# A delta rule before routed experts: chunks of 32 tokens with four heads on the partitions, the inverse by substitution on VectorE

## The chip, the core and the metric

One of the eight cores of a Trainium2 chip runs the whole program. The metric is the device time of one execution in microseconds (us), the median of three runs. A core has five engines with queues of their own: TensorE (PE; its weight loads are listed as PEld), VectorE (DVE), ScalarE (ACT), GpSimd (POOL) and SyncE (SP, which here only issues transfers). Each takes its instructions in order and waits at semaphores for the others.

## The reference

The first part is a linear attention with a delta rule, for 4 batch rows, 8 heads, 768 tokens and 48 columns a head; the second gives each of the 3072 tokens to one of 8 experts by a hash of its id. All is float32.

```python
k_n = k / (np.linalg.norm(k, axis=-1, keepdims=True) + 1e-06)
state = np.zeros((B, H, D, D))
for t in range(S):
    kt, vt, bt = k_n[:, :, t], v[:, :, t], beta[:, :, t, None]
    y[:, :, t] = np.einsum('bhd,bhde->bhe', q[:, :, t], state)
    v_old = np.einsum('bhde,bhd->bhe', state, kt)
    state = state + bt[:, :, :, None] * np.einsum('bhd,bhe->bhde', kt, vt - v_old)
x = y.transpose(0, 2, 1, 3).reshape(B * S, H * D)
expert_idx = token_ids * 2654435761 % E
for e in range(E):
    mask = expert_idx == e
    out[mask] = np.maximum(x[mask] @ w1[e], 0.0) @ w2[e]
```

## The kernel before, in words

**The delta rule** takes the tokens in chunks of 128. For one head and chunk, with L[t, s] = k_t . k_s for s < t and S0 the state ahead of the chunk, W solves (I + L diag(beta)) W = V - K S0; then Y = Q S0 + stril(Q K^T) diag(beta) W and S1 = S0 + (diag(beta) K)^T W. A unit is a chunk of one batch row with its 8 heads, and there are 24 units. Two generators work on a unit:

- `invert(n)` (L298) does what does not depend on the state. It normalises K on POOL (L308, L321), transposes K, Q and beta K on TensorE (L333), forms the two triangular products (L347, masked by VectorE at L350), and then builds the 128x128 inverse T of each head by doubling: six levels, from blocks of 2 rows to blocks of 128. A level is a product of all 8 heads into the PSUM tile `inv` (L367), masked by VectorE (L375), a second product evicted by ScalarE (L379), and a transpose (L372) evicted by ScalarE.
- `step(n)` (L403) does what depends on the state: psK = K S0 (L410), V - psK on VectorE (L418), W = T (V - K S0) (L423), the state's increment psS (L431), Y in psY (L410, L438), and the store of 128 token rows of Y to the DRAM tensor `x_scratch` (L447).

The loop at L456 interleaves two `invert` generators with one `step` and with the routing, which turns the token ids into the token of each expert slot (`gidx`). A scheduler then moves instructions between neighbouring stages, so an engine's final order is not the order of the code; each engine's queue keeps that final order.

**The experts** (L479 to L583) begin when the stores have landed. For each expert four indirect loads gather 128 token rows from `x_scratch` (L490), TensorE transposes them (L499), and two products with the expert's weights follow (L506 and L517); POOL scatters the rows (L521). Weights come by SP (L67, L69); the first expert's load stands at the middle of the delta rule, the next three behind its end.

The level of the doubling, which the change takes out, reads:

```python
Y = wk.tile([P, H, P], F32, tag="Y", bufs=2)
by_head(Y, product(LK, T), masked(i))
T = wk.tile([P, H, P], F32, tag="T", bufs=3)
by_head(T, product(TT, Y), copy)
TT = wk.tile([P, H, P], F32, tag="TT", bufs=3)
by_head(TT, transposed(T), copy)
```

## Time and profile before

| | |
|---|---|
| median of three runs | 1319.23 us (1318.14 to 1320.88) |
| the profiled execution: first to last instruction | 1317.1 us |
| what the median lies above that span | 2.1 us |
| TensorE matmul busy | 1268.8 us, 96% |
| TensorE weight loads busy | 1078.0 us, 82% |
| VectorE busy | 445.7 us, 34% |
| ScalarE busy | 403.9 us, 31% |
| GpSimd busy | 219.8 us, 17% |
| end of the delta rule's last eviction | 951.7 us |
| transfers | 54.94 MB, 42 GB/s over the span |

The profile is of one execution. The busy time of an engine is the union of its instructions; idle time is put down to whatever released the engine. The profiled execution's own device time is not listed apart from its span, so the span is compared with the median of the runs.

### The profile page before, as it was taken

To read this page: it belongs to the slowest core of one execution; us is meant where nothing else is said; L and a number is where in the kernel's file an instruction comes from. 1 tells how busy PE (TensorE), PEld (TensorE's weight loads), DVE (VectorE), ACT (ScalarE), POOL (GpSimd) and SP (SyncE) were. 2 spreads that over 40 slices of the span, in tenths; PEclk is the share of its full clock that TensorE was granted. 3 is DMA by queue.
4 is the path that set the end of the run, shared out by engine and by line. 5 is a ranking of instruction groups with operands and counts; after the bars stand their busy time and mean duration, and the time that the engine had idled before them with its cause. 6 is when DMAs were issued, how large, how long until landed. Compare 5 with 4: busy or idle time off the path is not lost. (4 is left out here: it accounts for less than half of the span.)

```text
span 1317.1 us, 20472 instructions
## 1 busy us (share of the span) xinstructions
PE 1268.8 (96%) x8730; PEld 1078.0 (82%) x8730; DVE 445.7 (34%) x926; ACT 403.9 (31%) x745; POOL 219.8 (17%) x214
## 2 busy tenths in 40 slices
PE   5899999999999999999999999999879999999997
PEld 4899999999999999999999999999835555555554
DVE  7734334343434443343444334333121111111110
ACT  1343444344343434434343443434300000000000
POOL 5402011110201111020111101011042211220011
PEclk9999999999999999999999999999979999999999
DMA  9001010111101011110100000000093232310000
GB/s 218 14 18 32 7 31 13 25 25 25 26 7 25 19 26 25 25 25 7 25 13 19 13 7 7 1 7 7 13 346 127 83 114 67 135 34 12 6 20 17
DMA packets 94236, 54.94 MB, mean 42 GB/s; under 512 B 77434, under 2 KB 88774, under 8 KB 94144
## 3 DMA queue, kind: packets, MB, share of 16 engines
q1 hardware_dynamic: 89856, 44.05, 12.4%
q0 software_dynamic: 4096, 9.45, 2.1%
q8 instruction: 69, 1.13, 0.4%
q14 instruction: 23, 0.19, 0.0%
q10 hardware_dynamic: 192, 0.12, 0.0%
HBM read 45.74 MB, written 11.01 MB: 43 GB/s over the span
## 5 line engine op out<-in xcount | busy, mean ns | idle before, releaser
L375 DVE TENSOR_TENSOR Y<-inv,masks 128x512 f32<-128x512 f32 x288 | 197.4, 691 | 254.0 <-PE inv L367 253.4
L367 PE MATMUL inv<-T,LK 128*128 128x128 f32 x2304 | 279.4, 276 | 3.0 <-DVE T L375 3.0
L367 PEld LDWEIGHTS inv<-T,LK 128*128 128x128 f32 x2304 | 268.3, 193 | 3.5 <-DVE T L375 3.5
L379 ACT ACTIVATE T<-inv 128x512 f32<-128x512 f32 x240 | 143.3, 597 | 343.1 <-PE inv L367 343.1
L367 PE MATMUL inv<-Y,TT 128*128 128x128 f32 x1920 | 235.7, 276 | 2.9 <-DVE Y L375 2.9
L367 PEld LDWEIGHTS inv<-Y,TT 128*128 128x128 f32 x1920 | 227.5, 192 | 5.9 <-ACT root L313 1.9
L517 PE MATMUL o_ps<-w_sb,h_sb 128*128 128x384 f32 x512 | 169.9, 486 | 0.0
L506 PE MATMUL h_ps<-xT,w_sb 128*128 128x512 f32 x384 | 168.0, 598 | 0.0
L506 PEld LDWEIGHTS h_ps<-xT,w_sb 128*128 128x128 f32 x384 | 73.7, 192 | 91.1 <-issue 89.2
L517 PEld LDWEIGHTS o_ps<-w_sb,h_sb 128*128 128x128 f32 x512 | 95.2, 190 | 61.1 <-issue 1.0
L379 ACT ACTIVATE TT<-inv 128x512 f32<-128x512 f32 x240 | 128.5, 600 | 28.7 <-PE inv L372 28.2
L372 PE MATMUL inv<-ident,T 128*128 128x128 f32 x960 | 122.7, 274 | 0.1
L321 POOL TENSOR_TENSOR KN<-Ku,rn 128x384 f32<-128x384 f32 x24 | 19.9, 828 | 555.3 <-PE psT L333 549.9
L372 PEld LDWEIGHTS inv<-ident,T 128*128 128x128 f32 x960 | 108.0, 143 | 1.7 <-ACT T L379 1.6
L347 PE MATMUL psG<-KQT,BT 128*128 128x256 f32 x384 | 95.3, 391 | 1.9 <-DVE LQ L350 1.1
L347 PEld LDWEIGHTS psG<-KQT,BT 128*128 128x128 f32 x384 | 70.0, 194 | 13.2 <-PE inv L367 1.1
L509 ACT ACTIVATE h_sb<-h_ps 128x512 f32<-128x512 f32 x32 | 19.1, 597 | 183.5 <-PE h_ps L506 162.4
L511 DVE TENSOR_SCALAR h_sb<-h_ps 128x512 f32<-128x512 f32 x32 | 22.1, 692 | 145.3 <-PE h_ps L506 145.3
L490 POOL DMA_INDIRECT xg<-x_scratch,gidx x32 | 32.7, 1021 | 208.4 <-PE xT_ps L499 151.2
L385 POOL TENSOR_TENSOR TT<-LK,mask_t 128x1024 f32<-128x1024 f32 x24 | 57.8, 2410 | 1.9
L521 POOL DMA_INDIRECT out_dram<-o_sb,gidx x32 | 32.0, 1001 | 136.4 <-ACT o_sb L520 87.4
L520 ACT COPY o_sb<-o_ps 128x384 f32<-128x384 f32 x16 | 7.6, 478 | 142.4 <-PE o_ps L517 142.4
(129 smaller groups left out, 1010.8 us busy)
## 6 DMA issues: line engine op xcount, KB each, us to landing
w_sb<-in_moe_w_dram SPq DMA_DIRECT2D x16, 1536.0 KB, 7.3
Ku<-in_k_dram SPq DMA_DIRECT2D x24, 192.0 KB, 3.2
Q<-in_q_dram SPq DMA_DIRECT2D x24, 192.0 KB, 3.4
Vu<-in_v_dram SPq DMA_DIRECT2D x24, 192.0 KB, 4.3
x_scratch<-x_sb SPq DMA_DIRECT2D x24, 192.0 KB, 1.9
xg<-x_scratch,gidx POOLq DMA_INDIRECT x32
out_dram<-o_sb,gidx POOLq DMA_INDIRECT x32
bt<-in_beta_dram ACTq DMA_DIRECT2D x1, 96.0 KB
```

What stands on the lines that cost most here:

```text
L321: nc.gpsimd.tensor_tensor(KN[:, :, 0:D], Ku, rn.broadcast_to([P, H, D]), op=ALU.mult)
L347: nc.tensor.matmul(psG[:, hh], lhsT=BT[:, j, hh, :], rhs=KQT[:, :, j, :], start=(hh == 0), stop=True, skip_group_check=True)
L367: return lambda ps, h, first: nc.tensor.matmul(ps, lhsT=lhsT[:, h, :], rhs=rhs[:, h, :], start=first, stop=True, skip_group_check=True)
L372: return lambda ps, h, first: nc.tensor.transpose(ps, t[:, h, :], ident)
L375: return lambda dst, ps: nc.vector.tensor_tensor(dst, ps, masks[:, i].broadcast_to([P, HB, P]), op=ALU.mult)
L379: nc.scalar.activation(dst, ps, ACT.Copy)
L385: nc.gpsimd.tensor_tensor(TT, LK, mask_t.broadcast_to([P, H, P]), op=ALU.mult)
L490: nc.gpsimd.indirect_dma_start(out=xg, out_offset=None, in_=x_dram[:, :], in_offset=bass.IndirectOffsetOnAxis(ap=idx, axis=0), bounds_chec ...
L506: nc.tensor.matmul(h_ps[:, :width], lhsT=w1_sb[:, co, fo * P:(fo + 1) * P], rhs=xT[:, co, :width], start=(co == 0), stop=(co == CO - 1))
L511: nc.vector.tensor_scalar(out=h_sb[:, fo, :width], in0=h_ps[:, :width], scalar1=0.0, scalar2=None, op0=ALU.max)
L517: nc.tensor.matmul(o_ps, lhsT=h_sb[:, fo, col * P:(col + 1) * P], rhs=w2_sb[:, fo, :], start=(fo == 0), stop=(fo == FO - 1))
L521: scat = nc.gpsimd.indirect_dma_start(out=out[:, :], out_offset=bass.IndirectOffsetOnAxis(ap=idx, axis=0), in_=o_sb, in_offset=None, bound ...
```

## The change

The delta rule is written anew, the experts are kept.

- A chunk is 32 tokens and holds all 32 (batch row, head) pairs: a tile of 128 partitions is four heads of 32 tokens, and there are NT = 8 such tiles a chunk and NU = 24 chunks. In K4 and Q4 (32 tokens x 4 heads on the partitions) a tile has two column blocks of 48, and a head fills the one of its parity, so that a product of K4 transposed serves two heads.
- `prepare(c)` loads and normalises K, transposes K4 and Q4 (16 transposes), adds column blocks on POOL (`side`), and makes in 8 matmuls the products with K and Q. The K products go by ScalarE into NT, the Q products masked by VectorE into MT. One bank, `psG`, holds them.
- `invert(g)` serves four chunks (GC = 4). A 32x32 block transpose on VectorE puts one (head, chunk) on each of the 128 partitions, with its 32x32 matrix along the free axis. Then 31 rounds of a multiplication into tmp and an addition to U build the inverse by substitution; a second block transpose gives TU.
- `step(c)` copies TU into the block diagonal TB, and takes two halves of four tiles through psK, R2, psW, W2, psS and psY. The state accumulates in PSUM (`psS`), and ScalarE copies it out after each half.
- Loads are four a tensor and chunk, each of 32 partitions; K has 7 buffers, Q and V 3. A chunk's rows are stored by four transfers. The rows of `x_scratch` stand in the order (token, batch row), and `gx` is the index tile for the gathers.
- beta comes by 16 small loads on POOL's queue. The first expert's weights are loaded when the last `prepare` is done.

The core of the diff:

```diff
-            for i in range(1, LEVELS):
-                Y = wk.tile([P, H, P], F32, tag="Y", bufs=2)
-                by_head(Y, product(LK, T), masked(i))
-                yield
-                if i < LEVELS - 1:
-                    T = wk.tile([P, H, P], F32, tag="T", bufs=3)
-                    by_head(T, product(TT, Y), copy)
-                    yield
-                    TT = wk.tile([P, H, P], F32, tag="TT", bufs=3)
-                    by_head(TT, transposed(T), copy)
-                    yield
...
+        for t in K4s[:4]:
+            nc.gpsimd.memset(t, 0.0)
...
+        for i in range(4):
+            for j in range(GC):
+                p0 = C * i + NT * j
+                nc.gpsimd.dma_start(out=beta_i[p0:p0 + NT], in_=beta_r[i, j])
...
+        def prepare(c):
+            K4, Q4 = K4s[c % NB], Q4s[c % 3]
+            if c >= 4:
+                load_k(c, nc.sync)
+            if c >= 3:
+                load_q(c, nc.sync)
+            ksq = pre.tile([P, NT, 2 * D], F32, tag="ksq", bufs=1)
+            nc.scalar.activation(ksq, K4.rearrange("p t r d -> p t (r d)"), ACT.Square)
...
+            nc.gpsimd.tensor_tensor(K4v, K4v, rn.broadcast_to([P, NT, 2 * D]), op=ALU.mult)
+            yield
+            for a, (src, dst) in enumerate(((K4, KTs[c]), (Q4, QTs[c]))):
+                for h in range(2):
+                    psT = ps_t.tile([2 * D, HT, P], F32, tag="t")
+                    for i in range(HT):
+                        nc.tensor.transpose(
+                            psT[:, i, :], src[:, HT * h + i].rearrange("p r d -> p (r d)"), ident)
+                    own = dst[:, HT * h:HT * h + HT]
+                    nc.scalar.activation(own, psT, ACT.Copy)
+                    by_r = own.rearrange("p t (u r c) -> p (t u) r c", u=2, r=2)
+                    nc.gpsimd.tensor_tensor(side[:, HT * h:HT * h + HT, a], by_r[:, :, 0],
+                                            by_r[:, :, 1], op=ALU.add)
+            yield
+            for h in range(2):
+                psG = ps_g.tile([P, 2, HT, 2 * C], F32, tag="g")
+                for i in range(HT):
+                    nc.tensor.matmul(
+                        psG[:, :, i, :], lhsT=KTs[c][:, HT * h + i],
+                        rhs=side[:, HT * h + i].rearrange("p a u c -> p a (u c)"),
+                        start=(i == 0), stop=True, skip_group_check=True)
+                for p in range(2):
+                    nc.scalar.activation(
+                        NTs[c // GC][pair(p), :, x0:x0 + HT].rearrange("p t x -> p x t"),
+                        psG[pair(p), 0, :, p * C:(p + 1) * C], ACT.Copy)
+                nc.vector.tensor_tensor(
+                    MTs[c][:, HT * h:HT * h + HT].rearrange("p t (u r c) -> p (t u) r c", u=2, r=2),
+                    psG[:, 1].rearrange("p t (u c) -> p (t u) c", u=2)[:, :, None, :]
+                    .to_broadcast([P, 2 * HT, 2, C]),
+                    mask.rearrange("p t (u r c) -> p (t u) r c", u=2, r=2), op=ALU.mult)
+                yield
+        def invert(g):
+            Ni = wk.tile([P, C, C], F32, tag="Ni", bufs=1)
+            nc.vector.transpose(Ni, NTs.pop(g))
+            nc.vector.tensor_tensor(Ni, Ni, nbeta[:, g, None, :].to_broadcast([P, C, C]),
+                                    op=ALU.mult)
+            U = wk.tile([P, C, C], F32, tag="U", bufs=1)
+            nc.gpsimd.memset(U, 0.0)
+            nc.gpsimd.tensor_copy(U.rearrange("p c i -> p (c i)")[:, ::C + 1], beta_i[:, g])
+            yield
+            for j in range(C - 1):
+                n, m = j + 1, C - 1 - j
+                tmp = wk.tile([P, C * C // 4], F32, tag="tmp", bufs=2, name="tmp")
+                tmp = tmp[:, 0:n * m].rearrange("p (n m) -> p n m", n=n)
+                nc.vector.tensor_tensor(tmp, U[:, 0:n, j:j + 1].to_broadcast([P, n, m]),
+                                        Ni[:, j:j + 1, j + 1:].to_broadcast([P, n, m]),
+                                        op=ALU.mult)
+                nc.vector.tensor_tensor(U[:, 0:n, j + 1:], U[:, 0:n, j + 1:], tmp, op=ALU.add)
+                yield
+            nc.vector.transpose(TUs[g].rearrange("p x i -> p i x"), U.rearrange("p c i -> p i c"))
+            yield
+        def step(c):
+            for i in range(4):
+                nc.vector.tensor_copy(TB[quarter(i), :, i, :], TUs[g][quarter(i), x0:x0 + NT, :])
+            yield
+            for h in range(2):
+                if c > 0:
+                    for i in range(HT):
+                        nc.tensor.matmul(psK[:, i], lhsT=KTs[c][:, t0 + i], rhs=S0[:, i],
...
+                for p in range(2):
+                        nc.vector.tensor_tensor(R2[pair(p), :, p], V[pair(p), t0:t0 + HT],
+                                                psK[pair(p), :, p], op=ALU.subtract)
...
+                for i in range(HT):
+                    nc.tensor.matmul(psW[:, i], lhsT=TB[:, t0 + i], rhs=R2[:, i],
...
+                nc.scalar.activation(W2, psW, ACT.Copy)
+                yield
+                if c < NU - 1:
+                    for i in range(HT):
+                        nc.tensor.matmul(psS[h][:, i], lhsT=K4s[c % NB][:, t0 + i], rhs=W2[:, i],
...
+                    nc.scalar.activation(S1, psS[h], ACT.Copy)
+                    states[h] = S1
+                yield
+                if c > 0:
+                    for i in range(HT):
+                        nc.tensor.matmul(psY[:, i], lhsT=QTs[c][:, t0 + i], rhs=S0[:, i],
...
+                for i in range(HT):
+                    nc.tensor.matmul(psY[:, i], lhsT=MTs[c][:, t0 + i], rhs=W2[:, i],
...
+        for c in range(NU):
+            todo = [step(c)]
+            if c + AHEAD < NU:
+                todo.append(prepare(c + AHEAD))
+                todo.append(parts(route, 1))
+            if c % GC == GC - 1:
+                todo.append(inv)
+            else:
+                todo.append(parts(inv, 12))
+            run(*todo)
+            if (c + AHEAD) % GC == GC - 1 and c + AHEAD < NU:
+                inv = invert((c + AHEAD) // GC)
```

The final order of three queues shows where the new work stands. On TensorE before, in the middle of the delta rule, the products of the inverse (`inv`, of one or the other of two units) surround the steps (psK, psW, psS, psY):

```order
L372 MATMUL inv<-ident,T 128x128 x8
L410 MATMUL psK<-Sbd,KQT 128x96 x4
L367 MATMUL inv<-T,LK 128x128 x8
L423 MATMUL psW<-Rn,last 128x48 x8
L367 MATMUL inv<-Y,TT 128x128 x8
L431 MATMUL psS<-W,BK_90 128x96 x4
L410 MATMUL psY<-Sbd,KQT 128x96 x4
L438 MATMUL psY<-W,LQ 128x48 x8
```

On TensorE with the change, around the first product with a new inverse (psW of chunk 12, which reads TB), stand only `prepare` of two later chunks (psT, psG) and the step itself:

```order
L433 MATMUL psK<-S_2752,KT 128x96 x4
L359 MATMUL psT<-ident,K_2_89 96x128 x8
L359 MATMUL psT<-ident,Q_1_102 96x128 x8
L375 MATMUL psG<-side,KT 128x2x64 x8
L444 MATMUL psW<-R_0_94,TB_98 128x96 x4
L461 MATMUL psY<-S_2752,QT 128x96 x2
```

What moved: the products of the inverse are gone from TensorE, and ahead of psW it has one `prepare` left to do. On VectorE with the change, the start of that same substitution, behind the last mask of the chunk that it waited for; before, VectorE had only masks and subtractions of single instructions here, such as `L375 TENSOR_TENSOR Y<-inv,masks 128x512 x6`:

```order
L384 TENSOR_TENSOR MT<-psG,mask 128x512
L394 STREAM_TRANSPOSE Ni<-NT 128x1024
L395 TENSOR_TENSOR Ni<-Ni,nbeta 128x1024
L437 TENSOR_TENSOR R_0_94<-V,psK 64x4x48
L405 TENSOR_TENSOR tmp<-U,Ni 128x31
L408 TENSOR_TENSOR U<-U,tmp 128x31
L405 TENSOR_TENSOR tmp<-U,Ni 128x60
L437 TENSOR_TENSOR R_0_94<-V,psK 64x4x48
L408 TENSOR_TENSOR U<-U,tmp 128x2x30
L405 TENSOR_TENSOR tmp<-U,Ni 128x87
```

A chain of 62 small instructions stands there now, with the subtractions of half a step inside it. On POOL with the change, the start of the program, where before a dozen memsets and the identity stood ahead of the first work on K:

```order
L116 MEMSET K_3_90 128x768
L153 DMA beta_i<-in_beta_dram 8x6x32 x16
masks.py:197 MEMSET ident 128x128
L165 MEMSET K_4_91 128x768
masks.py:199 ISA
masks.py:199 AFFINE_SELECT ident<-ident 128x128
L165 MEMSET K_5_92 128x768
L165 MEMSET K_6_93 128x768
```

Sixteen loads stand ahead of the identity now; seven more memsets and two index tiles (L167, L171) follow before the first normalisation of K (L348).

## Rows read from the trace of the kernel before

**Rows 1.** The page: busy us of the engines, TensorE's clock in 40 slices.

```profile
PE 1268.8 (96%) x8730; PEld 1078.0 (82%) x8730; DVE 445.7 (34%) x926; ACT 403.9 (31%) x745; POOL 219.8 (17%) x214
PEclk9999999999999999999999999999979999999999
```

**Rows 2.** Busy time by stage: stretch, us, each engine, clock, DMA share, GB/s.

```profile
0.00:952.00 952.00, 923.66 (x7738) 896.87 (x7738) 394.98 (x838) 377.14 (x697) 155.08 (x150) 1.00 0.11 24
952.00:1317.00 365.00, 345.14 (x992) 181.09 (x992) 50.73 (x88) 26.75 (x48) 64.72 (x64) 0.97 0.25 87
```

**Rows 3.** The same of instructions on the tile inv alone, first stage.

```profile
0.00:952.00 952.00, 678.69 (x5760) 657.34 (x5760) 228.34 (x336) 295.17 (x528) 1.00 0.11 24
```

**Rows 4.** Timeline of TensorE's weight loads: start us, us, line, operation, count.

```profile
601.34 1.78 PEld L372 LDWEIGHTS inv<-ident,T 128*128 128x128 f32 x16
603.09 3.65 PEld L367 LDWEIGHTS inv<-T,LK 128*128 128x128 f32 x32
606.66 3.65 PEld L367 LDWEIGHTS inv<-Y,TT 128*128 128x128 f32 x32
948.33 0.97 PEld L410 LDWEIGHTS psY<-Sbd,KQT 128*128 128x128 f32 x8
949.23 1.87 PEld L438 LDWEIGHTS psY<-W,LQ 128*128 128x128 f32 x16
```

**Rows 5.** Timeline of the last unit's hand-overs and last eviction.

```profile
945.88 0.56 DVE L418 TENSOR_TENSOR Rn<-Vu,psK 128x384 f32<-128x384 f32 x1 [1.73 <-PE psK L410]
946.55 1.86 PEld L423 LDWEIGHTS psW<-Rn,last 128*128 128x128 f32 x16 [0.87 <-ACT last L379]
948.58 0.49 ACT L426 ACTIVATE W<-psW 128x384 f32<-128x384 f32 x1 [2.52 <-PE psW L423]
951.25 0.49 ACT L445 ACTIVATE x_sb<-psY 128x384 f32<-128x384 f32 x1 [2.19 <-PE psY L438]
```

**Rows 6.** Groups by line and form: count, busy us, mean ns, idle before.

```profile
L249 DVE TENSOR_TENSOR rank<-rank,over 128x192 f32<-128x192 f32 x1 | 0.3, 345 | 0.0
L240 DVE TENSOR_TENSOR add_e<-ends,blocks 128x8 f32<-128x8 f32 x1 | 0.1, 149 | 0.0
L443 DVE TENSOR_TENSOR Sbd<-psS,Sbd 64x192 f32<-64x192 f32 x40 | 14.2, 355 | 75.2 <-PE psY L410 74.3 <-PE psS L431 0.7
L375 DVE TENSOR_TENSOR Y<-inv,masks 128x512 f32<-128x512 f32 x288 | 197.4, 691 | 254.0 <-PE inv L367 253.4
L310 DVE TENSOR_REDUCE ssq<-ksq 128x8 f32<-128x384 f32 x24 | 13.1, 545 | 0.0
L379 ACT ACTIVATE T<-inv 128x512 f32<-128x512 f32 x240 | 143.3, 597 | 343.1 <-PE inv L367 343.1
L321 POOL TENSOR_TENSOR KN<-Ku,rn 128x384 f32<-128x384 f32 x24 | 19.9, 828 | 555.3 <-PE psT L333 549.9 <-DVE rn L320 5.4
L385 POOL TENSOR_TENSOR TT<-LK,mask_t 128x1024 f32<-128x1024 f32 x24 | 57.8, 2410 | 1.9
L104 POOL MEMSET Sbd<- 128x1536 f32 x1 | 1.4, 1369 | 0.0
L490 POOL DMA_INDIRECT xg<-x_scratch,gidx x32 | 32.7, 1021 | 208.4 <-PE xT_ps L499 151.2 <-DVE xg L551 54.5 <-issue 1.8
```

**Rows 7.** Timeline of POOL and VectorE, 26 to 29 us.

```profile
26.17 2.37 POOL L385 TENSOR_TENSOR TT<-LK,mask_t 128x1024 f32<-128x1024 f32 x1
26.94 1.62 DVE L311 TENSOR_SCALAR ssq<-ssq 128x8 f32<-128x8 f32 x1
```

**Rows 8.** Busy time by stretch around the end of the delta rule.

```profile
952.00:960.00 8.00, 0.00 (x0) 0.00 (x0) 3.02 (x8) 0.00 (x0) 3.85 (x4) 0.68 0.64 222
960.00:972.00 12.00, 8.09 (x20) 4.39 (x21) 2.79 (x5) 0.00 (x0) 9.26 (x10) 0.50 1.05 384
```

**Rows 9.** Timeline of SP's queue at the start: the issue of 192 KB.

```profile
12.46 0.85 SPq L113 DMA_DIRECT2D Ku<-in_k_dram  x1
```

**Rows 10.** One group by line: eight rows of 24 elements.

```profile
L247 DVE TENSOR_TENSOR over<-over,add_e 128x192 f32<-128x192 f32 x1 | 0.3, 348 | 0.0
```

More of the change, by code (lines that the diff above doesn't have):

```diff
@@ L117 @@
-        bt = cst.tile([NBH, S], F32)
-        nc.scalar.dma_start(out=bt, in_=beta.rearrange("b h s -> (b h) s"))
-        for n in range(AHEAD):
-            load_unit(n)
-        tid32 = cst.tile([P, NTC, 2], I32)
+        NU = S // C
+        NT = B * H // 4
+        GC = 4
+        NG = NU // GC
+        AHEAD = 6
+        NB = AHEAD + 1
+        HT = NT // 2
+        st = phase1.enter_context(tc.tile_pool(name="st", bufs=1))
+        wk = phase1.enter_context(tc.tile_pool(name="wk", bufs=1))
@@ new lines, with rows, load_k, load_q @@
+        for t in Q4s:
+            nc.vector.memset(t, 0.0)
+        def rows(x):
+            return x.rearrange("b (g q) s d -> q s (b g) d", q=4)
+        k_r, q_r, v_r = rows(k), rows(q), rows(v)
+        def load_k(c, eng):
+            for i in range(4):
+                eng.dma_start(out=K4s[c % NB][quarter(i), :, i % 2, :],
+                              in_=k_r[i, c * C:(c + 1) * C])
+        def load_q(c, eng):
+            for i in range(4):
+                eng.dma_start(out=Q4s[c % 3][quarter(i), :, i % 2, :],
+                              in_=q_r[i, c * C:(c + 1) * C])
@@ new lines, with load_v @@
+        Vs = {}
+        def load_v(c):
+            Vs[c] = wk.tile([P, NT, D], F32, tag="V", bufs=3, name="V")
+            for i in range(4):
+                nc.sync.dma_start(out=Vs[c][quarter(i)], in_=v_r[i, c * C:(c + 1) * C])
+        for c in range(4):
+            load_k(c, nc.sync)
+        for c in range(2):
+            load_q(c, nc.scalar)
+        beta_i = st.tile([P, NG, C], F32)
+        beta_r = beta.rearrange("b (g q) (n c i) -> q c (b g) n i", q=4, c=GC, i=C)
+        for i in range(4):
+            for j in range(GC):
+                p0 = C * i + NT * j
+                nc.gpsimd.dma_start(out=beta_i[p0:p0 + NT], in_=beta_r[i, j])
@@ L122 @@
+        load_q(2, nc.scalar)
+        tid32 = rt.tile([P, NTC, 2], I32)
         tid_words = dataclasses.replace(moe_token_ids.tensor, shape=[N * 2], dtype=I32)
@@ L155 @@
[L155 to L164 removed]
+        nc.vector.tensor_scalar(out=row_i, in0=row_i, scalar1=C, scalar2=None, op0=ALU.is_lt)
@@ L366, in product @@
-            def product(lhsT, rhs):
-                return lambda ps, h, first: nc.tensor.matmul(
-                    ps, lhsT=lhsT[:, h, :], rhs=rhs[:, h, :], start=first, stop=True,
-                    skip_group_check=True)
-            def transposed(t):
-                return lambda ps, h, first: nc.tensor.transpose(ps, t[:, h, :], ident)
-            def masked(i):
-                return lambda dst, ps: nc.vector.tensor_tensor(
-                    dst, ps, masks[:, i].broadcast_to([P, HB, P]), op=ALU.mult)
@@ new lines, in run, with parts @@
+        def run(*its):
+            its = list(its)
+            while its:
+                for it in list(its):
+                    if next(it, its) is its:
+                        its.remove(it)
+        def parts(it, n):
+            for _ in range(n):
+                if next(it, it) is it:
+                    return
+                yield
+        route = routing()
+        for c in range(GC):
+            run(prepare(c))
+        inv = invert(0)
+        run(inv, prepare(GC))
+        for c in range(2):
+            load_v(c)
```

286 lines of the change are left out of this document (98 added, 188 removed).

## The prediction, made before the changed kernel had run

> **What bounds the kernel now.** The first view is the page's busy shares [rows 1]: TensorE works 1268.8 of 1317.1 us, no other engine more than 34%. The second, busy time by stage [rows 2], splits the span at the end of the delta rule. That end is the last eviction of the last unit, 951.25 + 0.49 = 951.7 us [rows 5]; the experts take the other 1317.1 - 951.7 = 365.4 us. In the first stage TensorE is busy 923.7 of 952 us, and 678.7 of these write the tile `inv` [rows 3]: the inverse by doubling is 71% of the stage, and the stage is TensorE's. A stretch of steady work then gives TensorE's prices, start to start of its weight loads [rows 4]: a transpose is one record, 16 in 601.34 to 603.09, 0.11 us each; any other matmul is two records, 32 records in 603.09 to 606.66, 0.22 us a matmul. Fewer columns are no cheaper: four 128x96 ones take 949.23 - 948.33 = 0.90 us.
>
> **The change, part by part.** The experts' stage is the same code (its row indices come from another small tile), so its 365.4 us stay. All the rest is the delta rule in a new form, and I price it as one stage: start, six substitutions on VectorE, and TensorE's spans between them.
>
> Prices first. VectorE, two operands in SBUF: 0.149 us for 8 elements a partition, 0.345 for 192 [rows 6], so 0.14 + 0.00107 n. From PSUM: 0.69 for 128x512, 0.355 for 64x192. ScalarE: 0.60 for 128x512, 0.49 for 128x384 [rows 5, 6]. POOL: 0.83 for 384 elements, 2.41 for 1024, so 0.51 for 256 and 1.78 for 768; a memset of 1536 takes 1.37 [rows 6]. A hand-over costs 0.25 us from TensorE to another engine (psW's last load ends its 1.78 us slot at 948.33, the eviction starts at 948.58) and 0.11 back (946.44 to 946.55) [rows 5].
>
> *TensorE's work.* A chunk of 32 tokens of all 32 heads costs 40 matmuls in `step` (8.9 us) and 16 transposes and 8 matmuls in `prepare` (1.8 + 1.8 = 3.6 us): 12.5 us, 24 times 299 us, where 924 stand now. So TensorE can no longer be the bound alone; waits will be.
>
> *A half of a step* (4 of the 8 tiles) is psK 0.9, hand-over 0.25, two subtractions 0.65, hand-over 0.11, psW 0.9, the Q S0 half of psY 0.9 (which just covers the eviction of W: 0.25 + 0.49 + 0.16), psS 0.9, the rest of psY 0.9: 5.45 us, 10.9 a chunk.
>
> *One substitution* has 62 VectorE instructions with sum 2 x n(32 - n) = 10912 elements a partition: 62 x 0.14 + 10912 x 0.00107 = 20.4 us; each needs the one before, 0.03 us more each, 22.2. Its two 32x32 transposes of 1024 elements and the scaling have no row; as an instruction of 1024 elements each is 1.2 us (between 0.69, the row of 512 from PSUM, and 2.41, POOL's row of 1024) [rows 6]. Sum 26 us. The Trainium skill speaks against this form (VectorE: DVE Perf Modes, "The TRN2 errata"): an instruction that reads SBUF pays a fixed latency of about 150 cycles, so small tiles should be avoided. By its 0.157 us instead of my 0.14 the six substitutions cost 6 us more; the row of 8 elements decides for 0.14.
>
> *What lies inside a substitution.* The order of VectorE puts the subtractions of the half steps, the norms and the masks of `prepare` between its instructions: a norm is a reduction of 768, twice 0.545, and six small ones at 0.149 [rows 6], 2 us. Groups 0, 1 and 2 hold two norms and two to five masks, 1 and 2 also six subtractions, 2 also routing (7, 8, 9 us); groups 3 and 4 one norm, two masks and two subtractions (4 each), the last two subtractions (1): 33 us. And POOL holds VectorE up: an instruction of 0.16 us took 1.62, until POOL's 2.37 us instruction had ended [rows 7]. POOL's share is 1.78 + 4 x 0.51 = 3.8 us a chunk; about five chunks of `prepare` fall inside substitutions, 20 us. All six: 6 x 26 + 33 + 20 = 209 us.
>
> *TensorE's spans between substitutions.* Substitution g+1 waits for `prepare` of chunk 4g+7, step 4g+4 waits for the substitution, and TensorE's order puts nearly all steps of a group ahead of that chunk's transposes. So the two alternate, and hardly overlap; that is the core of this forecast. Steps: 24 x 10.9 = 262; chunk 0 has no psK and no Q S0 (-6), chunk 23 no psS (-2); steps 3, 7 and half of 11 and five first psK lie inside substitutions (-27, -9): 218. Of the 17 later `prepare`, 11.5 lie here, 41 us. Routing's matmuls 5. Copies into TB, 4 x 0.3 after each substitution (a copy of 256 elements has no row; between 0.149, the shortest row, and 0.41 by the formula), 7. Each `prepare` also makes TensorE wait, for its one bank psG (0.25 + 0.69 + 0.11 twice, 2.1 us; 0 if other work covers it, 4 if POOL's normalisation of K is late too): 17 x 2.1 = 36. Sum 307 us.
>
> *The start.* The first transposes need the identity and a normalised K, which stand in POOL's queue behind four memsets (2.7 us from 1.0), 16 loads of beta, and ten memsets, the identity and two index tiles (7.1). A load issued by POOL has no plain row: an indirect one takes 1.02 [rows 6] and an SP issue 0.85 [rows 9]; I take 1.1 with the gap between two (0.4 to 1.3). So K 0 is normalised at 1 + 2.7 + 17.6 + 7.1 + 1.8 = 30 us. Two more normalisations, a fourth, four sums and the small things bring 40; then eight halves of `prepare` at 0.9 + 0.9 + 0.25 + 0.69 + 0.11 = 2.9 each, 23, and about 3 for the queues: the first substitution starts at 66 us.
>
> *The clock.* After the empty stretch 952 to 961 TensorE's granted clock was 0.50, its 1.2 GHz level, over 960 to 972, though it worked 8.1 of these 12 us [rows 8]. Each substitution leaves such a stretch behind, five in the loop; 12 us at half pace lose up to 6 us, partly inside waits: I take 3 each, 15 us (0 to 50).
>
> *Loads and stores.* Sixteen transfers of 48 KB a chunk replace three loads and a store of 192 KB a unit. A 192 KB load held SP's queue for 0.85 us [rows 9]; sixteen at that price are 14 us a chunk, under the (209 + 307)/24 = 21.5 us that a chunk lasts, so I price them at nothing. Without that cover they would be SP's bound.
>
> **Sum:** 66 + 209 + 307 + 15 = 597 us to the end of the delta rule, + 365.4 = 962 us of span. The median of the runs shown, 1319.23, stands 2.1 us above the profiled span: 965 us (1319 now).
>
> **The rivals.**
> 1. *The clock stays at 1.2 GHz.* TensorE would then work in bursts between waits and rarely be dense. The Trainium skill says so (TensorE: Matmul & The Clock Gate, "HAM oscillation"): a loop whose bursts alternate with long waits starts every burst at half clock. For it: [rows 8], and TensorE would work only some 275 of the loop's 516 us. Against it: 0.97 over the experts' stage that has that very gap [rows 2]. Price: the matmul part of the spans, some 220 us, twice: 965 - 15 + 220 = 1170 us. Chance 0.10.
> 2. *The pieces overlap.* If TensorE's waits for `prepare` are covered and POOL does not stand in VectorE's way, 36 and 20 us go; with the loads of beta at 0.4 another 11, and no loss to the clock 15: 965 - 82 = 883 us. For it: VectorE is free for most of the spans. Against it: [rows 7]. Chance 0.12.
> 3. *SP becomes the bound*: transfers of 32 partitions wait for each other, 2 us each. Then a chunk takes 32 us, 66 + 24 x 32 + 35 + 365 = 1235 us. Against it: 0.85 us for four times the bytes [rows 9]. Chance 0.04.
> 4. *Slower than before.* The updates write rows of m elements; if VectorE paid its fixed 0.14 us for every row instead of every instruction, a substitution has 992 rows, 139 us of fixed cost instead of 9: six times 130 more, 965 + 780 = 1745 us. It turns slower than before from 354/6 = 59 us a substitution, 0.06 us a row. Against it: eight rows of 24 took 0.348 us [rows 10], a flat 192 0.345 [rows 6]. Chance 0.02.
>
> That the inverse does not leave TensorE can be left out: the instruction lists show no product for it.
>
> **How the numbers follow.** Forecast 0.72, rivals 0.10, 0.12, 0.04, 0.02. The forecast's own bounds: down 11 (beta), 15 (clock), 36 + 20: 883, the second rival; up 3 (beta), 35 (clock), 32 (waits), 14 (transposes): 1049. I widen the top to 1085 for part of the first rival, and the bottom stays at 880; outside lie the rest of the first, the third and the fourth. About 0.2% can be told from no change; every case but the last is far faster: faster 0.97, same 0.01, slower 0.02.
>
> **What would show it.** The delta rule ending near 597 us and the first transpose of VectorE near 66; TensorE busy about 300 us before that end; each substitution 26 to 40 us with TensorE idle for most of it; the clock at 0.5 after each. If TensorE has no long idle stretch at the substitutions, the alternation is wrong; if the clock stays below 0.7 all through, rival 1 holds; if SP is the releaser of most waits, rival 3.

## The result and the profile after

The changed kernel takes 977.5 us (median of 4 runs, 976.9 to 979.3) where the kernel before takes 1319.0: a ratio of 0.741, 95% interval 0.740 to 0.742. The forecast was 965 us with a range of 880 to 1085. Below, a *window* is the time from the transpose into Ni (L394) to the end of the transpose into TU (L411), that is one substitution with all that VectorE does meanwhile; the *spans* are the stretches between windows.

The page's busy shares, in answer to [rows 1]; TensorE has lost 549 us of work, and no engine is near the whole span:

```profile
PE 719.4 (74%) x3684; PEld 528.1 (54%) x3684; DVE 388.9 (40%) x950; ACT 218.8 (22%) x479; POOL 200.2 (20%) x242
...
PEclk9975696599679956975689589599999999999998
```

The last eviction of the delta rule and, in the experts' stage, the first gather and the first matmuls [rows 5, 8]:

```profile
607.87 0.68 ACT L467 ACTIVATE x_sb<-psY 64x192 f32<-64x192 f32 x2 [1.24 <-PE psY L464]
...
614.12 1.18 POOL L532 DMA_INDIRECT xg<-x_scratch,gx  x1 [82.58 <-DVE xg L595]
...
620.48 0.90 PE L541 MATMUL xT_ps<-ident,xg 128*128 128x128 f32 x3 [12.64 <-DMA xg<-x_scratch,gx]
```

The delta rule ends at 608.5 us (951.7 before), and 369 us are left for the experts.

Busy time by stretch, in answer to [rows 2]: the start, then six windows and the spans behind them in turn, and the experts. Columns: stretch, us, busy us and instructions of TensorE's matmuls, its weight loads, VectorE, ScalarE and GpSimd, granted clock, DMA share, GB/s.

```profile
0.00:60.40 60.40, 22.50 (x144) 18.98 (x144) 30.09 (x67) 23.28 (x48) 41.88 (x71) 1.00 0.37 62
60.40:101.90 41.50, 19.15 (x80) 15.56 (x80) 36.50 (x86) 11.28 (x24) 9.59 (x11) 0.51 0.07 13
101.90:142.70 40.80, 34.02 (x252) 32.40 (x252) 20.31 (x63) 14.29 (x34) 8.38 (x8) 0.83 0.14 25
142.70:185.80 43.10, 26.77 (x145) 24.30 (x144) 36.68 (x90) 12.46 (x28) 9.43 (x10) 0.62 0.20 34
185.80:231.00 45.20, 37.83 (x306) 36.13 (x306) 17.27 (x46) 19.54 (x46) 9.71 (x12) 0.90 0.21 36
231.00:272.50 41.50, 20.16 (x137) 18.40 (x136) 34.86 (x91) 9.19 (x21) 4.96 (x5) 0.72 0.23 39
272.50:334.80 62.30, 51.09 (x415) 48.35 (x416) 22.72 (x67) 24.80 (x57) 14.08 (x17) 0.91 0.23 39
334.80:369.80 35.00, 10.64 (x59) 8.96 (x57) 31.31 (x77) 6.92 (x14) 4.55 (x5) 0.59 0.13 22
369.80:437.30 67.50, 54.76 (x416) 52.37 (x416) 21.26 (x58) 27.03 (x62) 14.13 (x17) 0.85 0.22 38
437.30:471.90 34.60, 7.90 (x32) 6.37 (x32) 31.25 (x78) 5.17 (x11) 4.56 (x5) 0.50 0.12 20
471.90:536.40 64.50, 54.12 (x416) 51.10 (x416) 20.34 (x58) 25.99 (x61) 14.06 (x17) 0.88 0.13 22
536.40:564.70 28.30, 0.03 (x1) 0.00 (x0) 26.11 (x68) 0.01 (x1) 0.00 (x0) 0.55 0.45 132
564.70:608.60 43.90, 35.27 (x296) 34.16 (x296) 9.50 (x31) 12.05 (x30) 0.00 (x0) 0.94 0.11 19
608.60:977.60 369.00, 345.19 (x992) 181.08 (x992) 50.72 (x88) 26.77 (x48) 64.86 (x64) 0.97 0.25 86
```

The windows sum to 224 us, the spans to 324, the start is 60. TensorE works 19 to 27 us of each of the first three windows, 11 and 8 us of the next two, and nothing in the last. Its longest waits:

```profile
PE psT L359 <- POOL K L348: 82.7, 17, 24.9
PE psW L444 <- DVE TB L422: 77.4, 6, 29.7
PE psW L444 <- DVE R L437: 33.5, 31, 3.0
```

The columns are total us, times, longest. The 24.9 is the start. The others of the first line lie mostly inside windows (9.0, 9.1, 12.6 and 16.0 us are the longest), the second line's at their ends. VectorE's last window, which shares the engine with nothing but two subtractions, shows what a substitution costs by itself (start, us):

```profile
536.35 1.24 DVE L394 STREAM_TRANSPOSE Ni<-NT 128x1024 f32<-128x1024 f32 x1
...
538.98 0.19 DVE L405 TENSOR_TENSOR tmp<-U,Ni 128x31 f32<-128x31 f32 x1
...
550.58 0.43 DVE L405 TENSOR_TENSOR tmp<-U,Ni 128x256 f32<-128x256 f32 x1
...
562.50 0.21 DVE L408 TENSOR_TENSOR U<-U,tmp 128x31 f32<-128x31 f32 x1
562.74 1.98 DVE L411 STREAM_TRANSPOSE TU<-U 128x1024 f32<-128x1024 f32 x1
```

It lasts 564.72 - 536.35 = 28.4 us, of which 0.7 are the subtractions; the 62 instructions take 23.3 of it.

### The profile page after: what moved, and what is told of

Its sections match the earlier page's. It is cut to its first block, busy times and chain, and to the rows that moved or that the text cites. A ratio compares the mean times of both kernels' runs of the same rounds, so it can differ in the third digit from the quotient of the medians.

```text
span 977.6 us, 10492 instructions
## 1 busy us (share of the span) xinstructions
PE 719.4 (74%) x3684; PEld 528.1 (54%) x3684; DVE 388.9 (40%) x950; ACT 218.8 (22%) x479; POOL 200.2 (20%) x242
## 5 line engine op out<-in xcount | busy, mean ns | idle before, releaser
L444 PE MATMUL psW<-R,TB 128*128 128x96 f32 x384 | 62.2, 309 | 111.9 <-DVE TB L422 77.4
L444 PEld LDWEIGHTS psW<-R,TB 128*128 128x128 f32 x384 | 54.9, 218 | 118.1 <-DVE TB L422 49.2
L359 PE MATMUL psT<-ident,K 128*96 128x128 f32 x192 | 39.1, 363 | 87.6 <-POOL K L348 82.7
L348 POOL TENSOR_TENSOR K<-K,rn 128x768 f32<-128x768 f32 x24 | 35.4, 1474 | 258.1 <-DVE rn L346 79.2
L375 PE MATMUL psG<-side,KT 96*128 96x128 f32 x384 | 66.7, 328 | 27.0 <-DVE MT L384 12.8
L375 PEld LDWEIGHTS psG<-side,KT 96*128 96x128 f32 x384 | 57.7, 230 | 35.2 <-issue 20.5
L405 DVE TENSOR_TENSOR tmp<-U,Ni 128x31 f32<-128x31 f32 (+15 forms) x186 | 73.9, 397 | 5.2
L408 DVE TENSOR_TENSOR U<-U,tmp 128x31 f32<-128x31 f32 (+15 forms) x186 | 72.5, 390 | 5.1
L464 PE MATMUL psY<-W,MT 128*128 128x96 f32 x384 | 55.8, 289 | 0.0
L461 PE MATMUL psY<-S,QT 96*128 96x96 f32 x368 | 55.4, 296 | 0.0
L381 ACT ACTIVATE NT<-psG 64x128 f32<-64x128 f32 x96 | 36.9, 384 | 77.7 <-PE psG L375 77.1
```

The lines of the kernel that those rows point to most:

```text
L359: nc.tensor.transpose(psT[:, i, :], src[:, HT * h + i].rearrange("p r d -> p (r d)"), ident)
L375: nc.tensor.matmul(psG[:, :, i, :], lhsT=KTs[c][:, HT * h + i], rhs=side[:, HT * h + i].rearrange("p a u c -> p a (u c)"), start=(i == 0), ...
L381: nc.scalar.activation(NTs[c // GC][pair(p), :, x0:x0 + HT].rearrange("p t x -> p x t"), psG[pair(p), 0, :, p * C:(p + 1) * C], ACT.Copy)
L405: nc.vector.tensor_tensor(tmp, U[:, 0:n, j:j + 1].to_broadcast([P, n, m]), Ni[:, j:j + 1, j + 1:].to_broadcast([P, n, m]), op=ALU.mult)
L408: nc.vector.tensor_tensor(U[:, 0:n, j + 1:], U[:, 0:n, j + 1:], tmp, op=ALU.add)
L444: nc.tensor.matmul(psW[:, i], lhsT=TB[:, t0 + i], rhs=R2[:, i], start=(i == 0), stop=True, skip_group_check=True)
```

## The experiments

They were to test the core of the forecast, that windows and spans alternate, so that each us of a window is a us of the kernel. All numbers are compared with 977.5 us (ratio to before 0.740 to 0.742).

**half_rounds**: half of the rounds are left out.

```diff
-            for j in range(C - 1):
+            for j in (*range(8), *range(23, C - 1)):
```

> Leaves out 15 of the 31 rounds of every substitution (rounds 8 to 22), so T is not the inverse; nothing else is changed. In the last substitution of the changed kernel, where nothing else runs, these 30 instructions stand from 544.43 to 558.43, 14.0 us. If substitutions and TensorE's spans alternate (the forecast's core), the time falls by six times that, 84 us, to some 893 us, a little less if work that stood between the rounds now stands in the way of the rest. If the pieces overlap, TensorE's own spans (324 us) already cover part of a substitution, and at most the waits named for TB, 77 us, of which half, can go: above 935 us.

Measured: 965.2 us (ratio 0.729 to 0.734). The expectation counts one round too many: rounds 8 to 22 end at 557.61 and not at 558.43, so 13.2 us are left out of a window, 79 in all and not 84. Of these only 12 came. Its windows do shrink, from 224 to 113 us in all, but its spans grow. Three stretches of it, the fifth window, the span behind it and the last window:

```profile
434.70:452.00 17.30, 3.47 (x16) 2.80 (x16) 16.29 (x45) 2.02 (x5) 2.20 (x2) 0.55 0.24 41
452.00:536.10 84.10, 65.70 (x434) 62.40 (x432) 22.85 (x59) 29.00 (x68) 16.09 (x20) 0.76 0.10 17
536.10:551.30 15.20, 0.00 (x0) 0.00 (x0) 14.04 (x38) 0.00 (x0) 0.00 (x0) 0.50 0.79 237
```

The last window begins at 536 as it did before the edit. The span ahead of it is 20 us longer than its counterpart (64.5): most of the transposes of a `prepare` that had stood inside the window are now behind it, the granted clock is 0.76 instead of 0.88, and TensorE is idle 18 us instead of 10. With shorter windows the scheduler had also made another order of the queues, so this run alone does not tell the window's price.

**half_same_order**: the same, with the order held. Each instruction is tied behind the one that stands ahead of it in the changed kernel's queue, by an edge that needs no semaphore. On TensorE, VectorE, ScalarE and GpSimd the trace shows the changed kernel's sequence of instructions in the delta rule, but for the 180 that are left out of VectorE's.

```diff
+            if _last is not None:
+                tc.add_manual_dep(_seq[_p], _last.name, mybir.DependencyInfo(
+                    mybir.DependencyClass.NoSync, mybir.DependencyReason.DATA), reason="order")
+            _last = _seq[_p]
```

> Leaves out rounds 8 to 22 of every substitution, as half_rounds did (T is not the inverse), but every engine keeps its queue in the order of the changed kernel, by ordering edges without a semaphore between neighbours. In half_rounds the scheduler had made another order, and the spans grew by what the substitutions lost. If the substitutions stand on the path in the order that was predicted for, TensorE's waits inside and behind them (psT for K's normalisation 9, 9, 13 and 16, psW for TB 3, 3, 17, 12, 12 and 30 us) shrink by up to 14 us each: 905 to 925 us. If TensorE's spans grow here too, by the clock or by waits that the rounds had covered, 945 us or more.

Measured: 952.1 us (0.720 to 0.724; the profiled execution 945.2), far short of 79. By its number this is the second expectation, but not by its reason: the spans grew by 5 us only (324 to 329). The windows last 36, 37, 36, 30, 30 and 15 us, 185 in all: only the last, without a `prepare`, gives the 13 us; the five others give 4.6 to 5.8. VectorE's queue in the fifth window shows why (in this kernel all recorded instructions carry line 123, so go by tiles):

```profile
413.13 1.23 DVE L123 STREAM_TRANSPOSE Ni<-NT 128x1024 f32<-128x1024 f32 x1
...
420.82 0.36 DVE L123 TENSOR_TENSOR U<-U,tmp 128x192 f32<-128x192 f32 x1
...
423.43 0.20 DVE L123 RECIPROCAL rn<-root 128x8 f32<-128x8 f32 x1
...
431.89 0.69 DVE L123 TENSOR_TENSOR MT<-psG,mask 128x512 f32<-128x512 f32 x1 [8.26 <-ACT NT L123]
435.44 0.69 DVE L123 TENSOR_TENSOR MT<-psG,mask 128x512 f32<-128x512 f32 x1 [2.85 <-ACT NT L123]
436.05 0.35 DVE L123 TENSOR_TENSOR tmp<-U,Ni 128x192 f32<-128x192 f32 x1
...
441.14 1.98 DVE L123 STREAM_TRANSPOSE TU<-U 128x1024 f32<-128x1024 f32 x1
```

The rounds stop at 421.2. The norm of the next chunk's K follows, and then two masks, for which VectorE waits 8.3 and 2.9 us, until GpSimd's normalisation, TensorE's transposes and products and ScalarE's evictions are through. The remaining rounds, ready since 421, stand behind them in the queue. In the changed kernel the rounds filled most of that time; its fifth window:

```profile
437.30 1.23 DVE L394 STREAM_TRANSPOSE Ni<-NT 128x1024 f32<-128x1024 f32 x1
...
463.38 0.69 DVE L384 TENSOR_TENSOR MT<-psG,mask 128x512 f32<-128x512 f32 x1 [1.44 <-ACT NT L381]
...
469.89 1.97 DVE L411 STREAM_TRANSPOSE TU<-U 128x1024 f32<-128x1024 f32 x1
```

There the last mask ends 26.8 us into the window, and 1.4 us is all that VectorE waits in it; with the rounds left out the mask ends 23.0 us in, after 11.5 us of waiting. In both cases 7 to 8 us of rounds and the last transpose stand behind it. In all six windows VectorE waits 16 us in the changed kernel and 60 here.

**half_no_norm**: the second chain is shortened. From half_same_order the normalisation of K is left out too, so that TensorE needn't wait for it inside a window.

```diff
-            nc.scalar.activation(ksq, K4.rearrange("p t r d -> p t (r d)"), ACT.Square)
-            nc.vector.tensor_reduce(ssq, ksq, axis=AX.X, op=ALU.add)
...
-            nc.vector.reciprocal(rn, root)
-            nc.gpsimd.tensor_tensor(K4v, K4v, rn.broadcast_to([P, NT, 2 * D]), op=ALU.mult)
```

> half_same_order (952 us) with the normalisation of K left out as well, its sum of squares, its small instructions and its product (K stays as loaded; T is not the inverse); all queues keep the changed kernel's order. In half_same_order the rounds lost 14 us a substitution, but the five windows from Ni's transpose to TU's that hold a prepare lost only 4.2 to 5.8, while the last, which holds none, lost 13.2. If the prepare inside the window is a second chain that keeps it open (TensorE waits 10 to 14 us in a window for the normalised K, and 12 us of its transposes, products and masks follow), the windows without that wait take 18 to 27 us, all six 130 to 145 us instead of 185, and the time is 870 to 900 us, a few us of it from an earlier start. If something else holds the windows open (VectorE's own instructions, GpSimd, TB), they stay above 165 us in all, and the time above 925 us.

Measured: 880.3 us (0.665 to 0.670), as the first expectation has it. Fifth window, the span behind it and the last window:

```profile
363.60:383.80 20.20, 5.42 (x26) 4.20 (x24) 15.90 (x41) 3.40 (x8) 3.80 (x4) 0.58 0.21 34
383.80:442.90 59.10, 50.09 (x416) 47.64 (x416) 14.25 (x36) 23.78 (x56) 9.72 (x14) 0.94 0.14 24
442.90:458.10 15.20, 0.11 (x1) 0.00 (x0) 13.97 (x38) 0.09 (x1) 0.00 (x0) 0.59 0.78 233
```

The windows sum to 146 us (185 with the normalisation), and VectorE waits 34 us in them. Its delta rule ends at 503.4 us, 71 earlier than in half_same_order (574.5): the windows give 39 of them, the start 12 and the spans 20. So it was `prepare` that held the shortened windows open. Up to the last mask in it a window lasts as long as the longer of two chains, VectorE's rounds ahead of that mask and the one or two `prepare`, which are tied together in VectorE's queue; the rounds behind the mask come on top. The normalisation alone, with all rounds kept, was not left out: what the second chain is worth by itself is not shown.

**prepare_first**: the scheduler takes prepare's instructions first.

```diff
-                todo.append(prepare(c + AHEAD))
+                todo.append(urgent(prepare(c + AHEAD)))
...
+        def urgent(it):
+            while True:
+                with tc.high_priority():
+                    if next(it, it) is it:
+                        return
+                yield
```

> Gives the instructions of prepare in the loop a higher priority for the scheduler; nothing else is changed. In TensorE's queue the last psG of a group then has 1.5 to 2.5 steps of the group before behind it, where 0 to 1 stood. If substitutions and TensorE's spans alternate because of that order, two steps (about 22 us) now lie beside each of the five later substitutions: 890 to 930 us, with TensorE busy for 20 us or more in each. If the steps' subtractions, which stand among the rounds on VectorE's queue, stretch the substitution by what the overlap gives, 950 to 980 us.

Measured: 976.8 us (0.736 to 0.743), no change, though TensorE now works 21 to 34 us in each later window. The windows grew to 241 us in all, and TensorE's waits went elsewhere:

```profile
PE psT L359 <- POOL K L348: 83.0, 16, 24.8
PE psW L444 <- DVE R L437: 67.2, 37, 10.3
PE psW L444 <- DVE TB L422: 22.2, 3, 14.0
```

The wait for TB fell from 77 to 22 us, the one for R rose from 34 to 67, some 35 of it inside windows (7 before): the steps now there wait for their subtractions in VectorE's queue. This is the second expectation. The overlap of TensorE's work is not in itself a gain.

**k_load_earlier**: K is loaded a chunk earlier, into eight buffers.

```diff
+        KB = 8
-            if c >= 4:
-                load_k(c, nc.sync)
+            if c >= 4 and c + 1 < NU:
+                load_k(c + 1, nc.sync)
```

> K gets an eighth buffer, and its load is issued a chunk earlier. The masks of the last chunk of a group end 22 us after that chunk's K load is issued (314.16 to 336.1), and the substitution waits for them. If the late load is what puts the substitution behind the steps, the substitutions begin up to a step earlier and five of them overlap TensorE's work by up to 11 us more: 920 to 960 us. If the order of the queues (VectorE's, where the norms of K stand among the rounds, and TensorE's) is what makes them alternate, a load that is there earlier changes little: 965 to 980 us.

Measured: 978.5 us (0.738 to 0.743), no change: the load is not what holds the windows back.

**warm_tensor**: TensorE is kept busy at the windows' ends.

```diff
+                for i in range({8: 74, 12: 54, 16: 52, 20: 130}.get(c, 0) if h == 0 else 0):
+                    nc.tensor.matmul(psW[:, i % HT], lhsT=MTs[c][:, i % HT],
+                                     rhs=K4s[c % NB][:, i % HT].rearrange("p r d -> p (r d)"),
+                                     start=(i % HT == 0), stop=True, skip_group_check=True)
```

> Ahead of the first psW of chunks 8, 12, 16 and 20, TensorE makes 74, 54, 52 and 130 more products into psW, which the real ones overwrite: 0.22 us each, as long as its waits for TB there (17.5, 12.3, 11.8 and 29.7 us). If the clock is lost on the path, as the forecast says (15 us; by the rows after the six substitutions TensorE works some 40 us at 1.2 GHz, so half of it, 20 us), four of the six give 8 to 13 us back, and the granted clock after these waits is near 1.0 from the first psW on. If TensorE's slower start is hidden by other waits, the time stays at 977; if the products overrun the waits it rises.

Measured: 983.7 us (0.744 to 0.747), 6 us slower, with a mean clock of 0.895 (0.854). The place of the products in the queue spoilt the test. TensorE around the last window:

```profile
535.04 30.35 PE L444 MATMUL psW<-K,MT 128*128 128x96 f32 x260
...
566.13 1.06 PE L433 MATMUL psK<-S,KT 96*128 96x96 f32 x8
...
572.75 2.66 PE L448 MATMUL psW<-R,TB 128*128 128x96 f32 x11 [5.57 <-DVE TB L422]
```

The products stood ahead of psK, whose subtraction stands among the rounds, so VectorE waited 5.7 us for it in this window, which lasted 34.7 us instead of 28.4. All windows together grew from 224 to 236 us, the spans fell from 324 to 317. In the spans, TensorE's busy time multiplied by one minus its granted clock, an estimate of what the clock takes away, stayed at 31 us: the higher mean clock is that of the windows, so what the clock costs on the path is not shown by this run.

**fill_r_wait and half_and_fill**: four more products follow each psK; the second kernel also leaves out the rounds of half_rounds.

```diff
+                if c > 0:
+                    for i in range(4):
+                        nc.tensor.matmul(psW[:, i % HT], lhsT=KTs[c][:, t0 + i % HT], rhs=S0[:, i % HT],
+                                         start=(i % HT == 0), stop=True, skip_group_check=True)
```

> Behind each psK, four more products of the same operands go into psW, which the real ones overwrite: 184 in all, 0.89 us a half step, about the 0.9 us that TensorE waits there for R. Nothing else is changed. With half of the rounds left out the time fell by only 12 us, and TensorE's granted clock was lower there (0.76 in the long spans against 0.85 to 0.91). If these waits bring the clock down, and the clock is on the path, the granted clock in the spans rises above 0.95 and up to 31 us come back (in the changed kernel's six spans, busy time by one minus the clock): 947 to 970 us. If the clock is not on the path, or the additional work costs as much as it gives, 975 to 1000 us.

Measured: 962.5 us (0.728 to 0.732), 15 us faster with 184 more products. In the spans, busy time by one minus the clock falls from 31 to 25 us, so by this estimate the clock accounts for 6; it is above 0.95 in one span of six only, not in all as expected. The scheduler also moved other products in this kernel (parts of psY ahead of psW, psK of the other half ahead of psS), as two_halves does below by intent, and the run does not separate that from the rest.

> Leaves out rounds 8 to 22 of every substitution (T is not the inverse) and has the four additional products of fill_r_wait. If TensorE's clock ate what the shorter substitutions should have given (in the spans of half_rounds, busy time by one minus the clock is 17, 14 and 16 us for the last three long ones), 30 to 55 us come back against 965: 910 to 935 us. If it is TensorE's own work that moved out of the substitutions into the spans, the time stays at 955 to 970 us.

Measured: 970.2 us (0.733 to 0.738): nothing came back. But the clock in the long spans was 0.77 to 0.81, little different from the 0.75 to 0.84 of half_rounds, so the run did not take the clock's loss away and doesn't price it. An estimate from half_rounds itself: its spans are 99 us longer than the changed kernel's (423 against 324), and busy time by one minus the clock grew from 31 to 66 us in them. So the clock can account for some 35 of the 99 us; the rest is work that had stood in the windows, and idle time.

**pool_to_dve**: GpSimd's part of prepare goes to VectorE.

```diff
-            nc.gpsimd.tensor_tensor(K4v, K4v, rn.broadcast_to([P, NT, 2 * D]), op=ALU.mult)
+            nc.vector.tensor_tensor(K4v, K4v, rn.broadcast_to([P, NT, 2 * D]), op=ALU.mult)
...
-                    nc.gpsimd.tensor_tensor(side[:, HT * h:HT * h + HT, a], by_r[:, :, 0],
+                    nc.vector.tensor_tensor(side[:, HT * h:HT * h + HT, a], by_r[:, :, 0],
```

> Moves the normalisation of K and the four additions into side from GpSimd to VectorE; same arithmetic. If a GpSimd instruction holds up VectorE for its whole length, the 21 us by which the substitutions' instructions are longer than their own shortest go, and some 13 us of new work (five chunks inside substitutions, each 0.96 for 768 elements and four times 0.41 for 256) come in: 5 to 15 us faster than 977. If GpSimd's work runs beside VectorE's for nothing, the new work is added to every substitution and to VectorE's part in the spans: 10 to 40 us slower.

Measured: 952.0 us (0.716 to 0.722), 25 us faster, more than expected and not where it was expected. The 21 us of stretched instructions are gone from the windows, yet these grew from 224 to 233 us with the work moved in. The start lost 5 us and the spans 29. A likely reason, not tested by itself: a `prepare` has fewer hand-overs, and 0.95 and 0.42 us on VectorE stand for 1.47 and 0.74 on GpSimd.

**two_halves**: a step takes both halves side by side, psK of both, then psW, psS and psY of both. **two_halves_pool** adds the edit of pool_to_dve.

```diff
-            for h in range(2):
-                t0 = HT * h
-                S0 = states[h]
-                R2 = R2s[(2 * c + h) % 4]
+            S0s, psWs, W2s = list(states), [None, None], [None, None]
+            R2c = [R2s[(2 * c + h) % 4] for h in range(2)]
+            for h in range(2):
+                t0 = HT * h
...
+            yield
+            for h in range(2):
+                t0 = HT * h
+                psW = ps_seq.tile([P, HT, 2, D], F32, tag="seq", name="psW")
```

> step does each stage for both halves before the next stage: psK of both, psW of both, psS of both, psY of both, where before one half ended ahead of the other. Same arithmetic. Each half's wait for R (33.5 us in 31 waits over 0.8) lies beside the other half's psK then. If TensorE's waits inside the steps, and the clock that falls after them, set the spans, 30 to 60 us go: 917 to 947 us. If the substitutions set the period, TensorE only waits longer for TB: 965 to 980 us.

Measured: 956.6 us (0.723 to 0.725), 21 us faster, between the two expectations: the windows lost 7 us and the spans 13. TensorE's waits, to be held against those of the changed kernel above:

```profile
PE psW L446 <- DVE TB L422: 76.1, 6, 28.7
...
PE psW L446 <- DVE R L437: 3.5, 7, 0.9
```

The waits for R are gone (33.5 to 3.5). The waits for TB in all are as long as they were.

> two_halves with GpSimd's part of prepare on VectorE, as in pool_to_dve, which took 25 us off. If the two gains are of different places they add: 25 less than two_halves. If VectorE is the bound once TensorE's waits are gone, the work moved to it gives nothing: the time of two_halves or above.

Measured: 922.3 us (0.697 to 0.700). Together the two edits give 55 us where they alone give 21 and 25.

**all_together** adds the edits of prepare_first and k_load_earlier, and four at the start:

```diff
-        for c in range(2):
-            load_q(c, nc.scalar)
+        for c in range(3):
+            load_q(c, nc.sync)
+        make_identity(nc, ident)
...
         for c in range(GC):
             run(prepare(c))
+        nbeta = st.tile([P, NG, C], F32)
+        nc.vector.tensor_scalar(out=nbeta, in0=beta_i, scalar1=-1.0, scalar2=None, op0=ALU.mult)
```

> two_halves_pool (922 us) with prepare first, K loaded a chunk earlier into an eighth buffer, Q's first loads on SP, the identity ahead of the loads of beta, and the scaling of beta behind the first norms. Three steps stand behind the last psG of a group. The start, 56 us there, loses the 4.5 us of the scaling and some 5 of the queues; each of four later substitutions can lie beside three steps of 9 to 11 us: 840 to 880 us. If VectorE, which now has all of prepare's additions, becomes the bound of the loop, above 900 us.

Measured: 919.9 us (0.696 to 0.699), not told apart from 922.3: the windows grew to 243 us and the spans fell to 247, and the start stayed at 58, where TensorE now waits 9.1 us for the load of Q. These last two are the fastest versions with the whole computation, 0.70 of the kernel before and 6% under the changed kernel.

## Why the prediction was right, and which step of it fell

The total was right to 12.5 us, and it was the likeliest case. The parts were off by -6 (start), +15 (windows), +2 (spans with the clock), +4 (experts) and -2 (what the median lies above the span), so part of the closeness is errors that cancel. Step by step:

- **The start**, 66, measured 60.4. A load of beta took 9.03 / 16 = 0.56 us on GpSimd, not 1.1. A piece the sum had not seen gave part of it back: the scaling of beta, 192 elements, took 4.46 us from 15.01 on, behind GpSimd's memsets, with the first norm queued behind it.
- **A substitution by itself**, 26, measured 27.7. Of the three long instructions the first two took 1.24 and 1.20 as taken, the transpose into TU 1.98. The 62 took 23.3, not 22.2: their own durations sum to 21.25, which less 10912 x 0.00107 is 0.154 us each, not the 0.14 I preferred, and 0.034 passes from one to the next. The Trainium skill's fixed latency of about 150 cycles (VectorE: DVE Perf Modes, "The TRN2 errata"), the 0.157 us of the prediction, agrees with this trace to 0.003 us.
- **What lies inside.** Interleaved work 33 (33 forecast), GpSimd's hold on VectorE 21 (20 forecast): 35 of the substitutions' instructions took over 0.3 us more than the shortest of their form, and all 35 ran beside an instruction of GpSimd. In the first window an instruction of 156 elements took 1.52 us, and 0.32 in the last; GpSimd's product ran from 68.97 to 70.44:

```profile
68.97 1.47 POOL L348 TENSOR_TENSOR K<-K,rn 128x768 f32<-128x768 f32 x1 [7.82 <-DVE rn L346]
69.09 1.52 DVE L405 TENSOR_TENSOR tmp<-U,Ni 128x156 f32<-128x156 f32 x1
```

  A term was missing: VectorE waits 16 us inside windows for masks and subtractions whose input is late. What is left of the sum, some 12 us, is saved where instructions begin before the one ahead has ended: 6 x 27.7 = 166, + 33 + 21 + 16 - 12 = 224, where the sum had 209.
- **TensorE's spans and the clock**, 307 + 15 = 322, measured 324. Two errors cancel here. By the rows above, busy time by one minus the clock is 31 us in the six spans, twice the 15 taken, and what is left, 293, is 14 under the 307. As forecast the clock is at 0.50, 1.2 GHz, after each window; it came back within 5 to 14 us (after the first window, which ends at 101.9, it is 0.50 until 114 and 0.76 over 114 to 118), so rival 1 did not come true: the spans' clocks are 0.83 to 0.94. The Trainium skill's "HAM oscillation" (TensorE: Matmul & The Clock Gate), by which a loop of bursts and long waits starts every burst at half clock, agrees with the start of each span here.
- **The work on both sides.** TensorE did 85 us in windows, by the clock's share 51 at full clock; the forecast had put 36 of steps and 5.5 `prepare`, 20 us, there. Of the signs that were named, TensorE was busy 374 us before the delta rule's end, not about 300 (310 at full clock); the windows lasted 28 to 43 us, not 26 to 40, and in the second TensorE was idle for 16 of 43 us, so not for most of it.
- **The experts**, 365.4, measured 369: the first gather begins 5.6 us behind the last eviction (3.5 before). The last chunk's rows go by four transfers now, which may be why; it was not tested. The median lies at the profiled span, not 2.1 above it: the profiled execution was the slowest of the four, 979.3 us, which is 1.7 above its own span.
- **The rivals.** Transfers were no bound: four issues of 48 KB took 1.9 to 3.1 us on SP's queue (308 to 318 us), so sixteen take some 9 of the 22.8 us that a chunk lasts. There is no price for a row: 16 rows of 16 took 0.42 to 0.43 us, where 0.14 + 0.00107 n gives 0.41. Overlap (rival 2) did not come by itself. Where TensorE's work was moved into the windows (prepare_first, 139 us there instead of 85) it gave nothing; where GpSimd's was moved to VectorE it gave 25 us, but in the spans and the start.

**The step that fell** is "All six: 6 x 26 + 33 + 20 = 209 us", taken as a price: that a window is a sum of the substitution and of what VectorE does between its rounds, so that each us less of rounds is a us less of the window. As an account of VectorE's time it holds to 15 us. The alternation in which it stands ("hardly overlap; that is the core of this forecast") holds too: TensorE is idle 16 to 28 us in each window, and with the order held 39 us less of windows brought the end of the delta rule 34 us forward (608.5 to 574.5, in the profiled executions). What the sum lacks is the `prepare` inside a window as a chain of its own, which ends at its last mask. With the order held, 13.2 us less of rounds took 4.6 to 5.8 off a window with a `prepare`, and 13.2 off the one without. The sum came near because with 31 rounds the two chains are nearly of one length, which the forecast did not look at and which is luck: in the fifth window the last mask ends 26.8 us in (437.3 to 464.1), and VectorE had waited 1.4 us for it. Left alone, the scheduler gave half of the gain back (965 against 952 us), in another order with a lower clock.

What stays open: how much of the 15 us of fill_r_wait is the clock's; what the normalisation alone would give with all rounds kept; and which queue ties the spans once `prepare` is first, since its waits were shown but not taken away.

## What to carry to other kernels

Time in which one engine works and the bound engine stands idle is not yet a price: look at what else in that window ends late, and which in-order queue holds both. Shorten one chain, then both, with the order of the queues held: 25 us against 97 (12 of them an earlier start) told more here than the sum did. Without the order held, the same edit to one chain gave 12, since the scheduler had made other queues. Work put into another engine's wait must be looked up in that engine's queue: it delays what stands behind it.

## What was not expected of the hardware

- The same block transpose of 128x1024 took 1.24 us between contiguous tiles (Ni) and 1.98 where both sides are read and written with a stride (TU).
- TensorE's clock also fell without a window: in half_rounds it went from 1.00 to 0.50 after a wait of 1.78 us for R (393 to 395 us), and stayed there some 7 us though TensorE worked throughout. After another wait of that length (ending at 498.6) it stayed at 1.00.
- Operands broadcast along either axis (column j of U, row j of Ni) cost VectorE nothing that shows: 256 elements took 0.43 us as a multiplication of two such operands, 0.42 as a plain addition.
